# Second up layer as seven quarter products, with DMA-made low halves and a deadline-ordered schedule, in an attention and two feed-forward layers kernel

## Chip, cores and metric

The kernel runs on one core of a Trainium2 chip. The metric is the device time of one execution in microseconds (us). Three runs of the kernel before took 534.87 to 536.11 us, with a median of 535.9 us. Engines are named as in the profile: PE is TensorE, DVE is VectorE, ACT is ScalarE, POOL is GpSimd, SP is SyncE, whose queue issues the plain DMAs.

## Reference

Attention with capped scores over 24 heads, then two feed-forward layers on 896 tokens of width 768, with 2048 hidden units each. All is in float32.

```python
scores = cap * tanh(q @ k.T / sqrt(64) / cap)       # 2 x 12 heads, 448 x 448, head_dim 64
x = softmax(scores) @ v                             # then tokens x 768
h = x @ w1; x = (max(h, 0) + alpha * min(h, 0)) @ w2    # first layer
h = x @ w3; out = max(h, 0) ** 2 @ w4                   # second layer
```

## The kernel before

Weights come from HBM as 64-bit floats and are rebuilt in 32 bits: ACT scales the high words (line 251), and DVE masks, shifts and joins the low words (lines 256, 258, 249). Where `half` is set, ACT does a part of it by a pass over the low words (line 245, on 16-bit halves), which takes the place of DVE's line 258.

TensorE multiplies in a rounded 32-bit format. For enough digits each operand is split into a high part h (ACT, line 275, rounds) and a low part l (DVE, line 276 or 277, what is left), and each product is three matmuls: h x h, h x l, l x h (line 210). All of these have 128 rows of weights and 448 columns of tokens, one of the two batches. `up_now` (line 218) already makes three blocks of the first up layer for one batch at the end of attention.

An up layer is a plain product: 16 blocks of 128 hidden units x 2 batches x 6 chunks x 3 matmuls. A down layer uses Winograd's form of Strassen's method. Weights and tokens are cut into 2 x 2 quarters (the two batches are halves of the tokens, the hidden units and outputs are halved too), and seven products of quarters P1 to P7 take the place of eight, at the price of sums: S1 to S4 of weight quarters, T1 to T4 of token quarters, and additions of the results. T4 and S4 are made by DMAs that accumulate into their destination, issued from POOL (`gather`, line 270).

The order of the work after attention is written out by a planner. `Plan.op` records every operation with an estimated cost, what it reads and what it writes. `Plan.order` then plays them through: whenever an engine is free, it starts the ready operation that was recorded first (lines 109, 125), if the buffers that it needs are free. Buffers come from pools by tag (`SLOTS`): `raw` for incoming weights, `w` for rebuilt weights, `wh` and `wl`, `xh` and `xl` for the split pieces, `g` for tokens, `ps` for PSUM banks. The result of the first layer goes into the tile `x` (`put`), high and low parts apart.

Of the kernel before, what the change touches and what calls it, by code (L numbers as in the profile page):

```python
# [32 lines left out]
PLAIN = ()  # L33

HALF = (lambda f, first: False, lambda i, a: i % 2 == 0)

SQ = lambda f: False

LAND = 9.0

SHIFT = 40

SHIFT_DOWN = 40

SLOTS = {"raw": 2, "w": 16, "wh": 3, "wl": 3, "g": 35, "t": 1, "xh": 4, "xl": 4}


class Buf:

    def __init__(self, tag=None, tile=None):  # L50
        self.tag, self.tile = tag, tile
        self.left, self.writer, self.readers, self.taken = 0, None, [], tag is None

# [9 lines left out]
class Plan:  # L63
# [4 lines left out]
    def tag(self, name, tiles):  # L68
        self.free[name], self.queue[name] = list(tiles), []

    def op(self, engine, cost, emit, reads=(), writes=(), port=False, lag=0.15):
# [7 lines left out]
        for other in set(before):  # L79
            if other is not None and other is not op:  # L80
                other.feeds.append(op)
                op.needs += 1
        for buf in reads:
            buf.readers.append(op)
        for buf in writes:
            buf.writer, buf.readers = op, []
            if not buf.taken:
                buf.taken = True
                op.takes.append(buf)
                self.queue[buf.tag].append(op)  # L90
        op.bufs = list(dict.fromkeys([*reads, *writes]))
        for buf in op.bufs:
            buf.left += 1

    def order(self):
        import heapq

        ready = {e: [] for e in {op.engine for op in self.ops}}
# [5 lines left out]
        while events:  # L104
            now = events[0][0]
            while events and events[0][0] <= now:
                _, _, what, op = heapq.heappop(events)
                if what == "ready":
                    heapq.heappush(ready[op.engine], (op.number, op))
                elif what == "end":  # L110
                    for buf in op.bufs:
                        buf.left -= 1
                        if not buf.left and buf.tag:
                            self.free[buf.tag].append(buf.tile)
# [5 lines left out]
            while moved:  # L120
                moved = False
                for e, waiting in ready.items():
                    if idle[e] > now:
                        continue
                    for item in sorted(waiting):
                        op = item[1]
                        if op.port and port > now:
                            continue
                        if any(self.queue[b.tag][0] is not op or not self.free[b.tag] for b in op.takes):
                            continue  # L130
                        for b in op.takes:
                            b.tile = self.free[b.tag].pop(0)
                            self.queue[b.tag].pop(0)
# [23 lines left out]
class Net:  # L157
# [47 lines left out]
    def multiply(self, ps, w, x, c, first, last, more=False):  # L205
        if len(w) == 1:
            self.nc.tensor.matmul(ps, w[0][:, c, :], x[0], start=first and not more, stop=last, skip_group_check=more)
# [23 lines left out]
    def load(self, src, half, sign=1):  # L231

        nc, plan, n = self.nc, self.plan, self.NC * P
        raw, w = Buf("raw"), Buf("w")
# [37 lines left out]
    def split(self, w, tags, n, sign=1):  # L272
        nc, plan = self.nc, self.plan
        h, l = (Buf(t) for t in tags)
        plan.op("ACT", self.act(n), lambda: nc.scalar.mul(h.tile, w.tile, -1.0) if sign < 0 else nc.scalar.copy(h.tile, w.tile), [w], [h])  # L275
        plan.op("DVE", self.dve(n), lambda: nc.vector.scalar_tensor_tensor(l.tile, w.tile, -1.0, h.tile.bitcast(F32), op0=ALU.mult, op1=ALU.subtract)
                if sign < 0 else nc.vector.tensor_sub(l.tile, w.tile, h.tile.bitcast(F32)), [w, h], [l], port=True)  # L277
        return h, l

    def products(self, ps, w, x, c, first, last, more=False):  # L280
        self.plan.op("PE", 3 * 0.2038 if len(w) == 2 else 0.746, lambda: self.multiply(ps.tile, [b.tile for b in w], [b.tile for b in x], c, first, last, more),
                     [*w, *x], [ps])

    def up(self, w, f, b, first):
# [3 lines left out]
        minus = b == 0 and f >= half  # L288
        for c in range(self.NC):
            self.products(ps, w, self.x[b, c], c, c == 0, c == self.NC - 1)  # L290
        if first or not minus:
            plan.op("ACT", self.act(S), lambda: nc.scalar.activation(g.tile, ps.tile, AF.Relu), [ps], [g])  # L292
        if first:
            plan.op("ACT", self.act(S), lambda: nc.scalar.activation(t.tile, ps.tile, AF.Relu, scale=-1.0), [ps], [t])
            slope = self.slope_t if minus else self.minus_t
            plan.op("DVE", self.dve(S), lambda: nc.vector.scalar_tensor_tensor(  # L296
                g.tile, t.tile, slope[:, f:f + 1], g.tile, op0=ALU.mult, op1=ALU.subtract if minus else ALU.add), [t, g], [g], port=True)
        else:
            if minus:
                plan.op("ACT", self.act(S), lambda: nc.scalar.mul(g.tile, ps.tile, -1.0), [ps], [g])  # L300
                plan.op("DVE", self.dve(S) + 0.06, lambda: nc.vector.scalar_tensor_tensor(
                    g.tile, ps.tile, 0.0, g.tile, op0=ALU.max, op1=ALU.mult), [g, ps], [g])
            elif SQ(f):
                plan.op("ACT", self.act(S), lambda: nc.scalar.square(g.tile, g.tile), [g], [g])
            else:
                plan.op("DVE", self.dve(S) + 0.06, lambda: nc.vector.scalar_tensor_tensor(
                    g.tile, ps.tile, 0.0, g.tile, op0=ALU.max, op1=ALU.mult), [g, ps], [g])
# [4 lines left out]
    def quarter(self, name, i):  # L312
        a = {"A11": 0, "S3": 1, "A12": 2, "A22": 3}[name]
        w = self.a[name, i] = self.load(self.wdown[:, a * PARTS + i], HALF[1](i, a), -1 if a == 2 else 1)
# [3 lines left out]
    def factor(self, name, i, plain):  # L318
# [8 lines left out]
        elif name == "S4":  # L327
            a[name, i] = a.pop(("A12", i))
            self.gather(a[name, i], a["S2", i])
        return (a[name, i],) if plain else self.split(a[name, i], ("wh", "wl"), n, -1 if name in ("S4",) else 1)  # L330

    def tokens(self, name, k, plain):
# [6 lines left out]
        elif name == "T4":  # L339
            self.gather(g[0, half + k], g[1, k])  # L340
# [530 lines left out]
```

## Time and profile before

| | |
|---|---|
| median of 3 runs | 535.9 us |
| profiled execution, its own time | 535.74 us |
| its span, first to last instruction | 534.0 us |
| PE busy | 517.3 us, 97% |
| DVE busy | 452.5 us, 85% |
| ACT busy | 343.0 us, 64% |
| granted TensorE clock | 0.999 of full speed |

The busy time of an engine is a share of the whole span; stages with different limits are mixed in it, so the section with rows below has a table by stage. A matmul's bar is longer than the distance to the next start, since matmuls overlap; the same holds for DVE and ACT when their queues are full. The distance between starts is then the price of an instruction.

### The profile page before, as it was taken

The numbers are of one execution on the slowest core, as the hardware profiler recorded it, in microseconds if no ns is written. First come the engines' busy times: TensorE is split into PE (matmuls) and PEld (weight loads), VectorE is DVE, ScalarE is ACT, GpSimd is POOL, SyncE is SP. The second block draws the span as 40 slices with busy tenths as digits, with TensorE's granted clock in tenths as the row PEclk, the third lists the DMA queues.
The fourth block names the chain that finished last, engine by engine and source line by source line (L and its number), as shares of the span: only waits on it lengthen the run. The fifth ranks groups of instructions, "written<-read, shape, count | busy, mean of one in ns | idle before, by whom it ended". The sixth has DMA issues, their size and how long they took to land.

```text
span 534.0 us, 7022 instructions
## 1 busy us (share of the span) xinstructions
PE 517.3 (97%) x2604; PEld 432.3 (81%) x2604; DVE 452.5 (85%) x639; ACT 343.0 (64%) x468; POOL 23.1 (4%) x36
## 2 busy tenths in 40 slices
PE   7889999999999999999999999999999999999995
PEld 2223335889999999789999989999999999999994
DVE  1598999878888989999999996987898999987661
ACT  5999994265568677975766734447756675556560
POOL 1000000000000000025000000000000001600000
PEclk9999999999999999999999999999999999999999
DMA  6545441044654455479201355556554500930111
GB/s 179 216 163 198 140 130 53 23 131 160 229 182 128 168 163 196 130 210 223 49 2 64 115 166 189 177 178 184 173 165 152 191 24 11 199 101 1 53 52 58
DMA packets 23034, 71.07 MB, mean 133 GB/s; under 512 B 4304, under 2 KB 13008, under 8 KB 22992
## 3 DMA queue, kind: packets, MB, share of 16 engines
q1 hardware_dynamic: 19392, 63.72, 36.4%
q0 software_dynamic: 3456, 6.82, 7.1%
q8 instruction: 22, 0.36, 0.3%
q14 instruction: 20, 0.16, 0.1%
q10 hardware_dynamic: 144, 0.00, 0.0%
HBM read 60.89 MB, written 2.79 MB: 119 GB/s over the span
## 4 chain that ended last, share of the span: by engine, by line
PE 67%; DVE 19%; ACT 8%; issue 3%; DMA 2%; POOL 0%; SPq 0%; DVEq 0%; ACTq 0%; POOLq 0%
PE hm L210 56%; PE pv L554 4%; PE ps L504 3%; DVE wl L277 3%; ACT raw L245 2%; DVE w L249 2%; PE ps L210 2%; DVE raw L258 2%; DVE xl L277 2%; ACT E L519 2%; DVE g L265 1%; ACT E L524 1%; DVE g L296 1%; DVE raw L256 1%; DMA v<-in_vT 1%
## 5 line engine op out<-in xcount | busy, mean ns | idle before, releaser
L210 PE MATMUL hm<-x,wh 128*128 128x448 f32 x732 | 205.5, 362 | 0.7 <-DVE x L352 0.5
L210 PEld LDWEIGHTS hm<-x,wh 128*128 128x128 f32 x732 | 137.2, 187 | 10.6 <-DVE x L352 0.8
L210 PE MATMUL hm<-x,wl 128*128 128x448 f32 x366 | 132.9, 363 | 0.6 <-DVE wl L277 0.6
L210 PE MATMUL hm<-xh,wh 128*128 128x448 f32 x336 | 122.2, 364 | 1.0 <-ACT g L361 1.0
L210 PE MATMUL hm<-xl,wh 128*128 128x448 f32 x336 | 122.2, 364 | 0.7 <-DVE xl L277 0.7
L210 PE MATMUL hm<-xh,wl 128*128 128x448 f32 x336 | 121.8, 363 | 0.0
L275 ACT CAST xh<-g 128x448 fp32r<-128x448 f32 x90 | 51.1, 569 | 53.6 <-PE hm L210 43.2
L277 DVE TENSOR_TENSOR wl<-w,wh 128x768 fp32r<-128x768 f32 x77 | 73.3, 952 | 5.9 <-ACT wh L275 4.8
L251 ACT ACTIVATE w<-raw 128x768 f32<-128x768 f32 x61 | 55.9, 916 | 33.2 <-DMA raw<-in_w 29.1
L275 ACT CAST wh<-w 128x768 fp32r<-128x768 f32 x77 | 64.4, 836 | 14.4 <-PE hm L210 10.7
L210 PEld LDWEIGHTS hm<-x,wl 128*128 128x128 f32 x366 | 68.7, 188 | 5.5 <-DVE wl L277 1.0
L249 DVE SCALAR_TENSOR_TENSOR w<-w,raw 128x768 int32<-128x768 int32 x61 | 58.1, 954 | 12.6 <-ACT raw L245 11.9
L210 PEld LDWEIGHTS hm<-xh,wh 128*128 128x128 f32 x336 | 63.1, 188 | 6.3 <-ACT g L361 2.0
L210 PEld LDWEIGHTS hm<-xl,wh 128*128 128x128 f32 x336 | 63.1, 188 | 5.8 <-DVE xl L277 1.7
L210 PEld LDWEIGHTS hm<-xh,wl 128*128 128x128 f32 x336 | 63.1, 188 | 4.2
L277 DVE TENSOR_TENSOR xl<-g,xh 128x448 fp32r<-128x448 f32 x90 | 55.3, 619 | 11.1 <-ACT xh L275 10.1
L292 ACT ACTIVATE g<-hm 128x448 f32<-128x448 f32 x53 | 29.4, 554 | 23.1 <-PE hm L210 23.1
L258 DVE SCALAR_TENSOR_TENSOR raw<-raw 128x768 int32<-128x768 int32 x45 | 42.9, 956 | 1.0
L519 ACT ACTIVATE E<-ps,scale_t 128x896 f32<-128x896 f32 x42 | 40.2, 1023 | 4.4 <-PE ps L504 4.3
L524 ACT ACTIVATE E<-E,cap_t 128x1792 f32<-128x1792 f32 (+1 forms) x24 | 38.2, 1620 | 0.0
L504 PE MATMUL ps<-q,k 64*128 64x448 f32 x132 | 30.4, 571 | 4.9 <-DVE rows L579 2.3
L245 ACT ACTIVATE raw<-raw 128x768 f16<-128x768 f32 x16 | 31.3, 1955 | 5.7 <-DVE raw L253 5.7
(89 smaller groups left out, 454.1 us busy)
## 6 DMA issues: line engine op xcount, KB each, us to landing
raw<-in_w SPq DMA_DIRECT2D x64, 768.0 KB, 4.2
g<-g POOLq DMA_DIRECT2D x16, 224.0 KB, 5.4
w<-w POOLq DMA_DIRECT2D x8, 384.0 KB, 6.2
out_T<-g SPq DMA_DIRECT2D x12, 224.0 KB, 2.0
k<-in_kT SPq DMA_DIRECT2D x11, 224.0 KB, 5.0
q<-in_qT SPq DMA_DIRECT2D x11, 224.0 KB, 5.5
v<-in_vT SPq DMA_DIRECT2D x6, 384.0 KB, 5.2
rb<-row SPq DMA_DIRECT2D x10, 224.0 KB, 3.7
```

The source lines that it names most:

```text
L210: self.nc.tensor.matmul(ps, a[:, c, :], m, start=first and n == 0 and not more, stop=last and n == 2, skip_group_check=more)
L245: nc.scalar.mul(halves[:, :, :, 1], parts()[1].bitcast(F32), sign * 2.0 ** -60)
L249: nc.vector.scalar_tensor_tensor(bits, bits, 3, parts()[0], op0=ALU.logical_shift_left, op1=ALU.bitwise_or)
L251: plan.op("ACT", self.act(n) + 0.06, lambda: nc.scalar.mul(w.tile, parts()[1].bitcast(F32), 2.0 ** -112), [high, raw], [w])
L258: plan.op("DVE", self.dve(n), lambda: nc.vector.scalar_tensor_tensor(parts()[0], parts()[0], 29, parts()[1], op0=ALU.logical_shift_right, ...
L275: plan.op("ACT", self.act(n), lambda: nc.scalar.mul(h.tile, w.tile, -1.0) if sign < 0 else nc.scalar.copy(h.tile, w.tile), [w], [h])
L277: if sign < 0 else nc.vector.tensor_sub(l.tile, w.tile, h.tile.bitcast(F32)), [w, h], [l], port=True)
L292: plan.op("ACT", self.act(S), lambda: nc.scalar.activation(g.tile, ps.tile, AF.Relu), [ps], [g])
L504: nc.tensor.matmul(ps[:, e, :], k[rows, c * P:c * P + P], q[rows], start=True, stop=True)
L519: nc.scalar.activation(es[-1][:, n % 2], ps, AF.Tanh, scale=self.scale_t)
L524: self.nc.scalar.activation(x, x, AF.Exp, scale=self.cap_t)
L554: nc.tensor.matmul(self.pv[u][rows, g, :], self.v[u][0][:, g, c, rows], self.chunk(u, g * FULL + c)[:, e], start=c == 0, stop=False)
```

## The change

The second up layer becomes seven products of quarters too (`squares`, `all_squares`), for each pair of a block and the block half the layer further on. The weights come in an order that fits (`quads`), and their quarters are combined on DVE (`weights`), but for the first sum of seven of the eight pairs, which is an accumulating DMA. The input of that layer is no longer put as is: `take` makes T1 to T4 and splits all seven token factors.

In `split`, a new way `far` makes the low half without DVE: ACT writes the rounded h and -x, also rounded, and an accumulating DMA adds x to it. T1 and T2 of both down layers go this way (`FAR`), and the four pieces of weight quarter A12 in the second (`FARW`). In the second down layer, T4 and S4 are sums on DVE (`T4`, `S4`).

The 16 raw blocks of the second up layer use ACT's low-word pass (`HALF`). There are three raw buffers; the scratch of software-made DMAs is 4096 bytes; buffers `cell` hold either a weight or two token halves, and the token pieces of the down layers use the slots of `x`.

The planner first plays the operations backwards in time (`rank`, `backwards`); the time at which each one would have to be done gives its place in the order, where the place in the recording stood before.

```diff
-HALF = (lambda f, first: False, lambda i, a: i % 2 == 0)
-LAND = 9.0
-SLOTS = {"raw": 2, "w": 16, "wh": 3, "wl": 3, "g": 35, "t": 1, "xh": 4, "xl": 4}
+GATHER = lambda k: k > 0
+HALF = (lambda f, first: not first, lambda i, a: i % 2 == 0)
+T4 = {False: True, True: False}
+S4 = {False: True, True: False}
+FAR = lambda final, name, k: name in ("T1", "T2")
+FARW = lambda final, name, i: final and name == "A12"
+SQUARE = lambda b, f: "ACT" if b else "DVE"
+LAND = 7.5
+SLOTS = {"raw": 3, "w": 9, "wh": 5, "wl": 5, "g": 35, "t": 1, "cell": 9}
...
     def order(self):
+        self.rank()
...
-                    heapq.heappush(ready[op.engine], (op.number, op))
+                    heapq.heappush(ready[op.engine], (op.rank, op.number, op))
...
-    def split(self, w, tags, n, sign=1):
+    def split(self, w, tags, n, sign=1, port=True, reads=None, far=False):
+        if far and sign > 0:
+            plan.op("ACT", self.act(n), lambda: nc.scalar.copy(h.tile, w.tile), reads, [h])
+            plan.op("ACT", self.act(n), lambda: nc.scalar.mul(l.tile, w.tile, -1.0), reads, [l])
+            self.gather(l, w)
+            return h, l
...
+    def take(self, name, j, x):
+        if name == "B12":
+            b11, b22, u = kept["B11", j], kept["B22", j], Buf("g")
+            plan.op("DVE", self.dve(S), lambda: nc.vector.tensor_sub(b11.tile, x.tile, b11.tile), [x, b11], [b11])
+            factor("T1", b11)
+            plan.op("DVE", self.dve(S), lambda: nc.vector.tensor_sub(u.tile, x.tile, b22.tile), [x, b22], [u])
+            factor("T3", u)
+            self.sum(b22, b22, b11, "tensor_sub", S)
+            factor("T2", b22)
+        else:
+            kept[name, j] = x
+            factor(name, x, 1 if name == "B21" else -1)
+            if name == "B21":
+                self.sum(x, x, kept["B22", j], "tensor_sub", S)
+                factor("T4", x)
+    def weights(self, src, k):
+        u0 = self.load(src[:, 2 * k], HALF[0](2 * k, False), -1)
+        u1 = self.load(src[:, 2 * k + 1], HALF[0](2 * k + 1, False))
+        a11, a12, a21, a22 = Part(u0, 0), Part(u0, 1), Part(u1, 0), Part(u1, 1)
+        if GATHER(k):
+            self.gather(a21, a11)
+        else:
+            self.sum(a21, a21, a11, "tensor_add", n // 2)
+        pairs["P1"] = pairs["P2"] = self.split(u0, ("wh", "wl"), n, reads=[a11, a12], far=DISTANT(k, "P1"))
+        pairs["P7"] = pairs["P4"] = self.split(u1, ("wh", "wl"), n, reads=[a21, a22], far=DISTANT(k, "P7"))
+        self.sum(a21, a21, a22, "tensor_add", n // 2)
+        pairs["P6"] = self.split(a21, ("wh", "wl"), n // 2)
+        self.sum(a12, a12, a21, "tensor_add", n // 2)
+        self.sum(a11, a21, a11, "tensor_sub", n // 2)
+        pairs["P5"] = pairs["P3"] = self.split(u0, ("wh", "wl"), n, reads=[a11, a12], far=DISTANT(k, "P5"))
+    def squares(self, k):
+        for name in ("P1", "P6", "P5", "P7", "P2", "P4", "P3") if LATE(k) else ("P1", "P2", "P6", "P5", "P7", "P4", "P3"):
+            c, at, b, more = parts[name]
+            p = ps[c]
+            for j in range(J):
+                self.products(p, self.pairs[k][name], self.factors[b, j], at * J + j, j == 0, j == J - 1, more)
+            if name in ("P1", "P6", "P7"):
+                keep(name, p)
...
-        self.raw = const.tile([P, 2, self.NC, P], I64, name="raw")
+        self.raw = const.tile([P, 3, self.NC, P], I64, name="raw")
...
-    nc = bacc.Bacc("TRN2", target_bir_lowering=False, num_devices=1)
+    nc = bacc.Bacc("TRN2", target_bir_lowering=False, num_devices=1, dynamic_dma_scratch_size=4096)
```

Three places show how instructions move. The first is DVE in the middle of the second up layer, before. `wl` is the low part of a weight block, `raw` and `w` are incoming and rebuilt weights, `hm` are PSUM banks and `g` the results.

```order
L306 SCALAR_TENSOR_TENSOR g4_795<-hm3_831,g4_795 128x448
L256 TENSOR_SCALAR raw_62<-raw_62 128x768
L306 SCALAR_TENSOR_TENSOR g6_797<-hm5_833,g6_797 128x448
L258 SCALAR_TENSOR_TENSOR raw_62<-raw_62 128x768
L249 SCALAR_TENSOR_TENSOR w10_785<-w10_785,raw_62 128x768
L256 TENSOR_SCALAR raw_62<-raw_62 128x768
L258 SCALAR_TENSOR_TENSOR raw_62<-raw_62 128x768
L277 TENSOR_TENSOR wl1_107<-w1_776,wh1_104 128x768
L306 SCALAR_TENSOR_TENSOR g3_794<-hm2_830,g3_794 128x448
```

And DVE in the same layer, now, with quarters of 384 columns:

```order
L374 SCALAR_TENSOR_TENSOR w4_783<-w4_783,raw_62 128x768
L499 TENSOR_TENSOR g22_810<-g22_810,hm0_823 128x448
L390 TENSOR_TENSOR w4_783<-w3_782,w4_783 128x768
L412 TENSOR_TENSOR wl3_111<-w0_779,wh3_106 128x768
L492 SCALAR_TENSOR_TENSOR g22_810<-g22_810 128x448
L412 TENSOR_TENSOR wl1_109<-w2_781,wh1_104 128x768
L518 SCALAR_TENSOR_TENSOR g24_812<-hm4_827,g24_812 128x448
L499 TENSOR_TENSOR g26_814<-g26_814,hm5_828 128x448
L499 TENSOR_TENSOR g20_808<-g20_808,hm0_823 128x448
L412 TENSOR_TENSOR wl0_108<-w6_785,wh0_103 128x768
L390 TENSOR_TENSOR g18_806<-g24_812,g18_806 128x448
L390 TENSOR_TENSOR w6_785<-w6_785 128x384
```

Where a block had one instruction on its result and one on its low part, there are now sums of weight quarters (line 390, 384 columns), joins of products (line 499) and squares (lines 492, 518) beside the low parts; the instruction of line 258 is gone from the blocks of this layer.

The second place is POOL's queue in the first down layer and after it. These are its accumulating DMAs before, from the last T4 on.

```order
L270 DMA g25_816<-g10_801 128x448
L270 DMA g27_818<-g12_803 128x448
L270 DMA w6_781<-w0_775 128x768
L270 DMA w7_782<-w2_777 128x768
L270 DMA w8_783<-w4_779 128x768
L270 DMA w9_784<-w0_775 128x768
L270 DMA g0_791<-g1_792 128x448
```

And now from the same T4 on; `x` are the slots of token pieces, here their low halves.

```order
L395 DMA g25_813<-g10_798 128x448
L395 DMA g27_815<-g12_800 128x448
L395 DMA x_63<-g0_788 128x448
L395 DMA x_63<-g1_789 128x448
L395 DMA x_63<-g2_790 128x448
L395 DMA x_63<-g4_792 128x448
L395 DMA x_63<-g6_794 128x448
L395 DMA x_63<-g8_796 128x448
```

Sixteen low halves of T2 and T1 are put behind the T4 in POOL's queue, and two of the four weight pieces of S4 come between the last of them.

The third place is PE where the two layers meet. Before, the last product of the first layer ran to its end, and the second layer's input `x` came after it. This is now; `cx` are token factors in `cell` buffers.

```order
L335 MATMUL hm4_827<-x_63,wl3_111 128x448
L335 MATMUL hm6_829<-x_63,wh3_106 128x448 x2
L335 MATMUL hm6_829<-x_63,wl3_111 128x448
L335 MATMUL hm7_830<-cx_2239,wh4_107 128x448 x2
L335 MATMUL hm7_830<-cx_2239,wl4_112 128x448
L335 MATMUL hm7_830<-cx_2252,wh4_107 128x448 x2
L335 MATMUL hm7_830<-cx_2252,wl4_112 128x448
L335 MATMUL hm7_830<-cx_2268,wh4_107 128x448 x2
L335 MATMUL hm7_830<-cx_2268,wl4_112 128x448
L335 MATMUL hm0_823<-cx_2355,wh2_105 128x448 x2
```

The first product of the second layer (into `hm7`) reads factors that were ready before; the next one (into `hm0`) reads a factor that `take` makes from the first layer's late results.

## Rows read from the trace of the kernel before

**Rows 1.** The page's head: span, busy time, share and instructions of an engine.

```profile
span 534.0 us, 7022 instructions
PE 517.3 (97%) x2604; PEld 432.3 (81%) x2604; DVE 452.5 (85%) x639; ACT 343.0 (64%) x468; POOL 23.1 (4%) x36
```

**Rows 2.** Busy time by stage: stretch, its length, busy us and instructions of each engine.

```profile
core 0: us, PE busy (x) PEld busy (x) DVE busy (x) ACT busy (x) POOL busy (x), PEclk, DMA share, GB/s
0.00:100.90 100.90, 93.49 (x499) 38.09 (x500) 79.94 (x98) 80.22 (x75) 2.02 (x12) 1.00 0.44 145
100.90:220.00 119.10, 118.50 (x593) 110.75 (x591) 104.27 (x145) 79.53 (x122) 0.00 (x0) 1.00 0.49 159
220.00:312.70 92.70, 90.24 (x444) 82.33 (x442) 91.76 (x143) 62.06 (x99) 10.63 (x12) 1.00 0.45 117
312.70:412.00 99.30, 99.30 (x496) 93.10 (x497) 84.49 (x120) 56.18 (x74) 0.00 (x0) 1.00 0.53 173
412.00:527.60 115.60, 115.60 (x578) 108.03 (x576) 91.13 (x136) 65.02 (x101) 10.42 (x12) 1.00 0.30 76
```

**Rows 3.** Timeline of PE: start, duration, line, operation, matmuls merged.

```profile
100.89 0.56 PE L210 MATMUL hm<-x,wh 128*128 128x448 f32 x2
...
517.64 0.36 PE L210 MATMUL hm<-xl,wh 128*128 128x448 f32 x1
...
527.44 0.36 PE L210 MATMUL hm<-xh,wl 128*128 128x448 f32 x1
```

**Rows 4.** The page's groups: the two layers' matmuls, count, busy, mean ns.

```profile
L210 PE MATMUL hm<-x,wh 128*128 128x448 f32 x732 | 205.5, 362 | 0.7 <-DVE x L352 0.5
L210 PE MATMUL hm<-x,wl 128*128 128x448 f32 x366 | 132.9, 363 | 0.6 <-DVE wl L277 0.6
L210 PE MATMUL hm<-xh,wh 128*128 128x448 f32 x336 | 122.2, 364 | 1.0 <-ACT g L361 1.0
L210 PE MATMUL hm<-xl,wh 128*128 128x448 f32 x336 | 122.2, 364 | 0.7 <-DVE xl L277 0.7
L210 PE MATMUL hm<-xh,wl 128*128 128x448 f32 x336 | 121.8, 363 | 0.0
```

**Rows 5.** Timeline of PE at two holes; in brackets idle time and releaser.

```profile
231.03 0.47 PE L210 MATMUL hm<-xl,wh 128*128 128x448 f32 x1 [0.65 <-DVE xl L277]
...
312.68 0.47 PE L210 MATMUL hm<-x,wh 128*128 128x448 f32 x1 [0.55 <-DVE x L352]
```

**Rows 6.** Timeline of DVE with a full queue.

```profile
261.62 0.62 DVE L265 TENSOR_TENSOR early<-g,g 128x448 f32<-128x448 f32 x1
262.16 0.95 DVE L277 TENSOR_TENSOR wl<-w,wh 128x768 fp32r<-128x768 f32 x1
263.03 0.62 DVE L277 TENSOR_TENSOR xl<-early,xh 128x448 fp32r<-128x448 f32 x1
```

**Rows 7.** Timeline of ACT with a full queue.

```profile
225.09 0.59 ACT L275 CAST xh<-g 128x448 fp32r<-128x448 f32 x1
225.56 0.86 ACT L275 CAST wh<-w 128x768 fp32r<-128x768 f32 x1
226.30 0.59 ACT L275 CAST xh<-g 128x448 fp32r<-128x448 f32 x1
...
230.69 1.95 ACT L245 ACTIVATE raw<-raw 128x768 f16<-128x768 f32 x1
232.38 0.90 ACT L275 CAST wh<-w 128x768 fp32r<-128x768 f32 x1
```

**Rows 8.** Accumulating DMAs: packets and MB, POOL's issue, time to landing of those on tokens.

```profile
q0 software_dynamic: 3456, 6.82, 7.1%
L270 POOL DMA_DIRECT2D g<-g x16 | 14.8, 966 | 8.6 <-DVE xl L277 7.6 <-issue 1.0
DMA to landing us min/median/max: 4.6/5.4/7.2
```

**Rows 9.** Waits in the second layer: total us, times, longest us.

```profile
DVE w L249 <- ACT raw L245: 8.6, 7, 2.0
```

More of the change, by code (lines that the diff above doesn't have):

```diff
@@ L89, in op, with rank @@
                 op.takes.append(buf)
-                self.queue[buf.tag].append(op)
+                self.queue[QUEUES.get(buf.tag, buf.tag)].append(op)
         op.bufs = list(dict.fromkeys([*reads, *writes]))
+        op.bufs += dict.fromkeys(b.whole for b in op.bufs if isinstance(b, Part))
         for buf in op.bufs:
             buf.left += 1
+    def rank(self):
+        count = {n: len(t) for n, t in self.free.items()}
+        claims, users = {}, {}
+        for op in self.ops:
+            op.later = list(op.feeds)
+            for b in op.bufs:
+                users.setdefault(id(b), []).append(op)
+        for op in self.ops:
+            for b in op.takes:
+                n = sum(count[p] for p in POOLS.get(b.tag, (b.tag,)) if p != "half")
+                c = claims.setdefault(b.tag, [])
+                if len(c) >= n > 0:
+                    for other in users[id(c[-n])]:
+                        if other.number < op.number:
+                            other.later.append(op)
+                c.append(b)
+        self.backwards()
@@ new lines, in backwards @@
+    def backwards(self):
+        import heapq
+        before = {}
+        for op in self.ops:
+            op.rank, op.open = 0.0, len(op.later)
+            for o in op.later:
+                before.setdefault(o, []).append(op)
+        now = {e: 0.0 for e in ("PE", "DVE", "ACT", "POOL", "SP")}
+        waiting = [(0.0, -op.number, op) for op in self.ops if not op.open]
+        heapq.heapify(waiting)
+        ready = {e: [] for e in now}
+        due = {op: 0.0 for op in self.ops}
+        left, time = len(self.ops), 0.0
+        events = [(0.0, -1)]
+        while left:
+            while waiting and waiting[0][0] <= time:
+                op = heapq.heappop(waiting)[2]
+                heapq.heappush(ready[op.engine], (-op.number, op))
+            for e, r in ready.items():
+                if r and now[e] <= time:
+                    op = heapq.heappop(r)[1]
+                    span = 1.8 if e == "SP" else op.cost
+                    now[e] = time + span
+                    op.rank = -(time + op.cost)
+                    left -= 1
+                    for o in before.get(op, ()):
+                        due[o] = max(due[o], time + op.cost + o.lag)
+                        o.open -= 1
+                        if not o.open:
+                            heapq.heappush(waiting, (due[o], -o.number, o))
+            times = [t for t in now.values() if t > time]
+            if waiting:
+                times.append(max(waiting[0][0], time + 1e-9))
+            time = min(times)
@@ L206, in multiply @@
         if len(w) == 1:
-            self.nc.tensor.matmul(ps, w[0][:, c, :], x[0], start=first and not more, stop=last, skip_group_check=more)
+            self.nc.tensor.matmul(ps, w[0][:, c, :], x[0], start=first, stop=last)
             return
@@ L287, in up @@
         ps, g, t = Buf("ps"), Buf("g"), Buf("t")
-        minus = b == 0 and f >= half
+        minus = T4[False] and b == 0 and f >= half
         for c in range(self.NC):
             self.products(ps, w, self.x[b, c], c, c == 0, c == self.NC - 1)
[L291 to L307, printed above, removed]
@@ L357, in down @@
         kept, chains = {}, {}
+        self.ring = "z" if final else "x"
         def keep(name, j, ps):
```

258 lines of the change are left out of this document (188 added, 70 removed).

## Prediction

> **What bounds the kernel now.** I read the profile from the top: the busy shares, then a table by stage, then the matmuls' own starts, then what fills VectorE and ScalarE. TensorE is busy 97% of a span of 534.0 us and VectorE 85% [rows 1]. The table by stage says where each matters [rows 2]. The first 100.9 us are attention. From there to 312.7 us runs the first feed-forward layer, to 527.6 us the second, and the last 6.4 us write the output. In the second layer TensorE is full (99.3 of 99.3 us, 115.6 of 115.6) while VectorE works 84.5 + 91.1 = 175.6 of 214.9 us and ScalarE 56.2 + 65.0 = 121.2. Between 220 and 312.7 us it is the other way round: VectorE is busy 91.8 of 92.7 us and TensorE has gaps.
>
> A busy TensorE can still be slower than its peak, so I take the pace from the starts. From the matmul at 517.64 us to the one at 527.44 us there are 49 steps [rows 3]: 9.80 / 49 = 0.200 us each. The two layers hold 732 + 366 + 3 x 336 = 2106 of them [rows 4], which is 421.2 us without a gap. They start at 100.89 us and the last one ends its step at 527.64 us, 426.75 us later. So 5.5 us are holes: by the counts of the stages almost all lie before 312.7 us (444 matmuls are 88.8 of 92.7 us). Two of them show their cause: TensorE waits for VectorE's low half of a token piece at 231.03 us, and for the next layer's input at 312.68 us [rows 5].
>
> **The change, part by part.** *Matmuls.* The second up layer was 16 blocks x 2 batches x 6 chunks x 3 = 576 matmuls. As seven products it is 8 pairs x 7 x 3 chunks x 3 = 504. Nothing else changes their number: 2106 - 72 = 2034. That is 72 x 0.200 = 14.4 us off the path that sets the end, since TensorE is full in that layer.
>
> *VectorE.* By the built order, from before to after, instructions on 448 columns go up by 13, those on 768 go down by 8, and 33 on 384 columns are new. The price of one in a full queue is the distance between starts, 0.535 us for 448 columns and 0.87 us for 768 [rows 6]; 384 columns were not run before, and the straight line through the two gives 0.47 (ends: 0.43, in proportion to 448 columns, and 0.535, the 448-column price itself). Sum: 7.0 - 7.0 + 15.5 = +15.5 us. Split by place: the first layer loses 16 low halves of token pieces to DMAs (-8.6 us), but where 12 low halves were made for the next layer's input, there are now 21 and 12 sums (33 against 12, +11.2 us). The second layer gets 8 x 0.535 - 8 x 0.87 + 33 x 0.47 = +12.8 us. It saves 16 instructions on 768 columns (raw weights are now joined with ScalarE's help) and 16 low halves, and pays for sums and splits of weight quarters, joins and squares.
>
> *ScalarE.* 57 more on 448 columns, 12 more on 768, 8 on 384, and 16 more passes that shift the low word of raw weights. Starts lie 0.47, 0.74 and 1.69 us apart [rows 7], 0.40 estimated for 384: 27 + 9 + 3 + 27 = +66 us, of which 32 x 0.47 + 9 + 3 + 27 = 54 us fall in the second layer.
>
> So in the second layer, where the work takes 214.9 - 14.4 = 200.5 us of TensorE, VectorE needs 175.6 + 12.8 = 188.4 us and ScalarE 121.2 + 54 = 175. All of this lies beside the matmuls as long as no queue runs empty waiting for another. The cover shrinks, though: VectorE's idle time there goes from 39.3 us to 12.1 us, and the transition's 11.2 us come right in front of it.
>
> *Accumulating DMAs.* There were 24 and are now 55; 36 of these make the low half of a piece (ScalarE writes -x, rounded, and the DMA adds x). Those of before on 448 columns took 4.6 to 7.2 us from issue to landing, 5.4 in the middle, and GpSimd 0.97 us to issue [rows 8]. The kind with a rounded destination isn't in the trace; its bounds are those 4.6 and 7.2 us, and I take 5.4. On the path it costs nothing: the token pieces go round in a ring of 24 slots, 12 pieces of a high and a low half, and each piece is read by 9 matmuls, so a slot comes free 11 x 9 = 99 matmuls, 20 us, before TensorE reads what is put there next. ScalarE's two steps (0.94 us), the issue and the landing are 7.3 us. Even 12 us more would be hidden; beyond that each late piece would hold TensorE by its whole excess.
>
> The scratch for these DMAs shrinks to 4096 bytes. The trace has 3456 packets for the 24 of before [rows 8], 144 each, 9 on each of 16 DMA engines; by the built order each waits for the eighth before it, so eight are in flight at most. [...]
>
> *Third raw buffer, attention.* One weight load can start earlier. The first 100.9 us are full with attention's own work (TensorE 93.5, ScalarE 80.2 us) [rows 2]; I take 0, with ends of 0 and -7.4 us (all that TensorE isn't busy there).
>
> *New order.* The holes can go either way. Those between 220 and 312.7 us arise with a full VectorE, which now has 8.6 us less to do there: I expect 1.5 of the 3.9 us to stay. In the second layer VectorE goes from 82% to 94% (188.4 / 200.5), and the transition makes its first part fuller still. When VectorE was as full as 99%, TensorE lost 3.9 us in 92.7 us. At half that rate, 200.5 us lose 4.2 us; I take 4.5. With 0.5 us at the start: 6.5 us of holes in place of 5.5. Ends: 0 and 12 us (the full-VectorE rate over the whole second layer, 8.4 us, and the 3.9 us unchanged).
>
> **The sum.** The profiled execution took 535.74 us, 1.7 us beyond its span, and the median of the runs is 535.9 us, practically the same, so I count from 535.9: - 14.4 (72 matmuls) + 1.0 (holes 6.5 for 5.5) = 522.5 us.
>
> **The rivals.**
> First, the new order closes the holes. All three engines have less work than TensorE in each layer, which speaks for it; that VectorE has only 12 us left speaks against it. With 0 to 4 us of holes: 535.9 - 14.4 - 5.5 = 516.0 up to 520 us.
>
> Second, and on the other side: VectorE becomes the second layer's bound through its waits for ScalarE's low-word pass. Such a pass takes two steps of a full VectorE, and the join of the same weights stands behind it in VectorE's queue. In the second layer of before VectorE waited for it 7 times, 8.6 us in all, 1.2 us each [rows 9], with 8 passes; now there are 24 (all 16 blocks of the second up layer, 8 of the down layer). If each still costs 1.1 us, that is 26 us, plus 11.2 us spilled over from the transition, against 12.1 us of idle time: 25 us of new holes, 521.5 + 25 = 546 us. It makes the kernel slower from 14.4 us of new holes on, which is 0.64 us of waiting per pass. For it: 1.2 us was paid where VectorE had 39 us to spare. Against: a wait that fills otherwise idle time is not a price, and the new order sorts by when a result is due, so other work can stand between. A half-way form, 6 to 13 us of new holes, gives 528 to 534 us.
>
> Third, the change of scratch doesn't leave the DMAs free: each would wait for the one before. The low halves are due every 9 matmuls, 1.8 us, and one after another they would take 5.4 + 1 us: 32 x 4.6 = 147 us less two leads of 20 us, 107 us, so 629 us. [...]
>
> **How the numbers follow.** My forecast (4 to 12 us of holes, 520 to 528 us) has 0.52; closed holes (516 to 520, a little under if attention gains) 0.24; the half-way form 0.12; the second rival in full 0.07; the third 0.02; and 0.03 is left for a result within 0.3% of 535.9 us (534.3 to 537.5), which is about what a measurement can tell from no change. So faster 0.52 + 0.24 + 0.12 = 0.88, same 0.03, slower 0.09. The range from 516 to 530 us leaves out the slow cases and a third of the half-way form.
>
> **What would show it right or wrong.** In the profile after, 2034 matmuls of the two layers, 0.200 us apart in the full stretches; VectorE near 468 us and ScalarE near 410 us busy; landing of the low halves near 5 us, and no wait of TensorE for a DMA. Holes are to lie in the 50 us after the layers meet, with a wait for VectorE. If TensorE loses over 12 us there, and VectorE's longest waits are for the low-word pass, the second rival holds. If gaps lie between GpSimd's DMAs in the first down layer, or TensorE waits for them, it is the third. A span below 514 us would mean that attention itself got shorter, which I count as nothing.

## The result and the profile after

The changed kernel takes 523.1 us (median of 4 runs, 522.25 to 524.66) where the kernel before takes 536.0: a ratio of 0.976, 95% interval 0.972 to 0.980. The forecast was 522.5 us. The profiled execution after took 523.51 us with a span of 521.6.

The page's head of the changed kernel, which answers to [rows 1]:

```profile
span 521.6 us, 7032 instructions
PE 505.3 (97%) x2532; PEld 419.1 (80%) x2532; DVE 459.8 (88%) x677; ACT 402.8 (77%) x561; POOL 51.4 (10%) x67
```

TensorE has 72 instructions less, ScalarE works 59.8 us longer, VectorE only 7.3 us. By stage, in the stretches of [rows 2] (stretch, its length, busy us and instructions of each engine, granted clock, share of the DMA engines, GB/s):

```profile
0.00:100.90 100.90, 93.45 (x498) 37.88 (x499) 80.06 (x98) 79.64 (x75) 2.02 (x12) 1.00 0.47 153
100.90:220.00 119.10, 119.10 (x597) 111.36 (x595) 110.62 (x157) 91.37 (x136) 0.00 (x0) 1.00 0.57 186
220.00:312.70 92.70, 89.30 (x445) 82.98 (x444) 84.38 (x135) 78.66 (x123) 27.14 (x30) 1.00 0.65 141
312.70:412.00 99.30, 98.46 (x474) 88.99 (x474) 94.95 (x151) 81.17 (x111) 4.71 (x5) 0.98 0.51 153
```

Attention is as long as it was. VectorE does 110.6 us of work between 100.9 and 220 us instead of 104.3, and has less in the stretch after it. The pace and the holes come from the starts of the two layers' matmuls; here they are by form, with count, least, median and longest duration in ns, and first and last start:

```profile
L335 PE MATMUL hm<-x,wh x1212: 360/362/576, 101.0 to 516.4; 128*128 128x448 f32 x174
L335 PE MATMUL hm<-x,wl x606: 360/363/575, 101.4 to 516.6; 128*128 128x448 f32 x152
L335 PE MATMUL hm<-cx,wh x144: 360/363/474, 306.4 to 420.3; 128*128 128x448 f32 x144
L335 PE MATMUL hm<-cx,wl x72: 360/363/525, 306.8 to 420.5; 128*128 128x448 f32 x72
```

The four counts add up to 2034. From 101.0 us to the end of the last step at 516.8 are 415.8 us; 2034 x 0.200 are 406.8, so 9.0 us are holes, against 5.5 before. Slower steps count as holes here. After the last start there are 5.0 us until the span ends, 6.6 before [rows 1, 3]. Together: -14.4 (matmuls) + 3.5 (holes) - 1.6 (tail) + 0.1 (a later start) = -12.4 us, which is the difference of the spans.

Of the two holes of [rows 5] the first is gone: TensorE is busy 20.00 of 20 us in each window from 220 to 300 us. Where the layers meet there is a larger one. PE's timeline there (start, duration, line, operation, in brackets idle time and releaser):

```profile
308.00 0.36 PE L335 MATMUL hm<-cx,wl 128*128 128x448 f32 x1
309.89 0.67 PE L335 MATMUL hm<-cx,wh 128*128 128x448 f32 x2 [1.52 <-ACT wh L410]
312.44 0.47 PE L335 MATMUL hm<-cx,wl 128*128 128x448 f32 x1 [1.88 <-DVE wl L412]
...
314.82 0.57 PE L335 MATMUL hm<-x,wl 128*128 128x448 f32 x1
315.19 0.95 PE L335 MATMUL hm<-x,wh 128*128 128x448 f32 x2
```

TensorE lacks the first weight blocks of the second up layer, then runs with steps of 0.37 us instead of 0.20 until 317.3 us. In the windows of 2 us from 312 us on the granted clock is 0.95, 0.50 and 0.70, and 1.00 again from 318 us, with no gap left after 312.44 us.

```profile
312.00:314.00 2.00, 1.56 (x7) 1.48 (x8) 2.00 (x4) 0.48 (x2) 0.00 (x0) 0.95 0.00 0
314.00:316.00 2.00, 2.00 (x7) 1.75 (x7) 2.00 (x4) 0.24 (x1) 0.00 (x0) 0.50 0.00 0
316.00:318.00 2.00, 2.00 (x9) 1.82 (x8) 2.00 (x4) 0.80 (x2) 0.88 (x1) 0.70 0.86 246
```

So some 3.8 us of gaps and 1.6 us of slow steps, 5.4 of the 9.0 us, lie within 12 us of the meeting at 306.4 us. VectorE is busy 19.9 of 20 us from 280 to 300 us. But before that it stood still, as these windows show:

```profile
240.00:260.00 20.00, 20.00 (x101) 18.75 (x100) 18.23 (x27) 18.12 (x33) 14.02 (x16) 1.00 1.11 213
260.00:280.00 20.00, 20.00 (x101) 18.75 (x100) 13.59 (x21) 17.54 (x23) 0.97 (x2) 1.00 0.69 175
```

VectorE is idle 8.2 of these 40 us. The longest wait, 3.7 us, is for a raw weight load, which was issued at 258.61 us and took 9.5 us to land, where the median of all loads is 4.3. The other 4.5 us are waits for ScalarE, which makes h and -x of each piece whose low half a DMA finishes and is busy 18.1 and 17.5 of 20 us here. VectorE's timeline:

```profile
263.96 0.62 DVE L411 SCALAR_TENSOR_TENSOR x<-g,x 128x448 fp32r<-128x448 f32 x1
268.24 0.56 DVE L378 TENSOR_SCALAR raw<-raw 128x768 int32<-128x768 int32 x1 [3.66 <-DMA raw<-in_w]
```

From 240 to 260 us, up to the issue of that load, GpSimd is at work on 16 accumulating DMAs, and the DMA engines' share is 1.11. The queue and the landing of the DMAs on tokens, answering to [rows 8]:

```profile
q0 software_dynamic: 7920, 13.70, 15.1%
L395 POOL DMA_DIRECT2D x<-g x28 | 25.5, 1110 | 19.7 <-ACT x L403 17.1 <-DVE w L374 0.9 <-issue 0.7
DMA to landing us min/median/max: 3.1/5.1/10.0
```

### The profile page after: what moved, and what is told of

It is laid out like the page before. It is cut to its first block, busy times and chain, and to the rows that moved or that the text cites. A ratio compares the mean times of both kernels' runs of the same rounds, so it can differ in the third digit from the quotient of the medians.

```text
span 521.6 us, 7032 instructions
## 1 busy us (share of the span) xinstructions
PE 505.3 (97%) x2532; PEld 419.1 (80%) x2532; DVE 459.8 (88%) x677; ACT 402.8 (77%) x561; POOL 51.4 (10%) x67
## 4 chain that ended last, share of the span: by engine, by line
PE 40%; DVE 33%; ACT 14%; issue 7%; DMA 6%; POOL 0%; DVEq 0%; ACTq 0%; POOLq 0%
PE hm L335 31%; DVE wl L412 5%; ACT raw L370 4%; DMA raw<-in_w 4%; DVE x L412 4%; DVE raw L383 3%; PE pv L797 3%; DVE w L374 3%; DVE g L390 3%; PE ps L335 2%; ACT w L376 2%; DVE cw L390 2%; PE ps L747 2%; ACT wh L410 2%; DVE g L541 2%
## 5 line engine op out<-in xcount | busy, mean ns | idle before, releaser
L335 PE MATMUL hm<-x,wh 128*128 128x448 f32 x1212 | 342.3, 363 | 0.7 <-ACT g L487 0.7
L335 PEld LDWEIGHTS hm<-x,wh 128*128 128x128 f32 x1212 | 227.6, 188 | 18.1 <-ACT g L487 2.6
L335 PE MATMUL hm<-x,wl 128*128 128x448 f32 x606 | 220.1, 363 | 0.0
L335 PEld LDWEIGHTS hm<-x,wl 128*128 128x128 f32 x606 | 114.1, 188 | 8.0 <-DVE wl L412 0.3
L370 ACT ACTIVATE raw<-raw 128x768 f16<-128x768 f32 x32 | 62.9, 1965 | 3.2 <-DVE raw L378 2.9
L410 ACT CAST x<-g 128x448 fp32r<-128x448 f32 x77 | 41.8, 567 | 10.9 <-DVE g L390 9.3
L412 DVE TENSOR_TENSOR x<-g,x 128x448 fp32r<-128x448 f32 x77 | 47.4, 618 | 0.3 <-ACT x L410 0.2
L335 PE MATMUL hm<-cx,wh 128*128 128x448 f32 x144 | 41.1, 366 | 1.7 <-ACT wh L410 1.5
L390 DVE TENSOR_TENSOR g<-g,g 128x448 f32<-128x448 f32 x55 | 33.3, 619 | 0.1
L747 PEld LDWEIGHTS ps<-q,k 64*128 64x128 f32 x132 | 10.9, 185 | 23.9 <-ACT E L762 11.2
L797 PE MATMUL pv<-E,v 128*64 128x448 f32 x144 | 29.5, 546 | 0.1
```

The source lines that it names most:

```text
L335: self.nc.tensor.matmul(ps, a[:, c, :], m, start=first and n == 0 and not more, stop=last and n == 2, skip_group_check=more)
L370: nc.scalar.mul(halves[:, :, :, 1], parts()[1].bitcast(F32), sign * 2.0 ** -60)
L390: plan.op("DVE", self.dve(n), lambda: getattr(nc.vector, op)(out.tile, a.tile, b.tile), [a, b], [out], port=True)
L410: plan.op("ACT", self.act(n), lambda: nc.scalar.mul(cut(h), w.tile, -1.0) if sign < 0 else nc.scalar.copy(cut(h), w.tile), reads, [h])
L412: if sign < 0 else nc.vector.tensor_sub(cut(l), w.tile, cut(h).bitcast(F32)), [*reads, h], [l], port=port)
L747: nc.tensor.matmul(ps[:, e, :], k[rows, c * P:c * P + P], q[rows], start=True, stop=True)
```

## The experiments

My theory after the result (A): the hole at the meeting comes from the accumulating DMAs of the first down layer, which delay the raw load, so that VectorE idles and is late afterwards. Its rival (B): VectorE simply has too much to do there. Beside that, each part of the change was undone alone. "Holes" is worked out as above from the starts in each run's profiled execution; that was the fastest of its runs for e1 (519.8 us) and e3 (534.9 us) and the slowest for e8 (525.2 us) and e11 (538.8 us), so a difference of 2 or 3 us in this column alone says little.

| run | edit | us | ratio to before (95%) | holes, us |
|---|---|---|---|---|
| changed kernel | | 523.1 | 0.976 (0.972 to 0.980) | 9.0 |
| e1 | no DMAs for low halves, first down layer | 521.2 | 0.975 (0.970 to 0.979) | 5.9 |
| e2 | VectorE makes them instead | 523.9 | 0.976 (0.974 to 0.979) | 8.9 |
| e3 | plain second up layer | 537.4 | 1.004 (1.001 to 1.007) | 6.4 |
| e4 | order as written | 543.0 | 1.014 (1.011 to 1.017) | 26.1 |
| e5 | half the DMAs, passes alternate | 519.5 | 0.970 (0.968 to 0.972) | 5.6 |
| e6 | no low-word pass, second up layer | 526.9 | 0.983 (0.980 to 0.985) | 12.4 |
| e7 | two raw buffers | 535.3 | 0.999 (0.998 to 1.001) | 20.3 |
| e8 | no DMAs for T1, T2 at all | 523.9 | 0.977 (0.974 to 0.979) | 11.2 |
| e9 | e5 with later up weights | 519.5 | 0.969 (0.967 to 0.971) | 4.7 |
| e10 | before with three raw buffers | 535.2 | 0.9972 (0.9949 to 0.9995) | 5.5 |
| e11 | e7 and e6 together | 536.8 | 1.000 (0.999 to 1.002) | 23.7 |
| e12 | scratch of 512 bytes | 602.1 | 1.122 (1.119 to 1.125) | 88.4 |

**e1, the DMAs left out.**

```
-            self.gather(l, w)
+            if self.ring == "x":
+                plan.op("POOL", 1.3, lambda: None, [w, l], [l], lag=LAND)
+            else:
+                self.gather(l, w)
```

> The changed kernel in its order, with 32 accumulating DMAs left out: those that finish the low halves of T1 and T2 pieces in the first down layer (the low half stays -x, so the result is another one). VectorE's and ScalarE's instructions stay the same. Theory A (the hole of 5.5 us where the layers meet comes from these DMAs: a raw weight load issued at 258.6 us takes 9.5 us to land beside them, VectorE idles 8 us between 240 and 280 us and runs late after that): raw loads land in under 6 us there, VectorE is busy over 18.5 of each 20 us from 240 to 280, the hole is under 2 us, time 517 to 520 us. Theory B (VectorE simply has too much to do before the layers meet, the late load hides nothing else): the hole stays 4 to 6 us, time 522.5 to 524.5 us.

Sixteen DMAs are left out, half of the 32 that the expectation names: those of the second down layer stay. The loads issued between 240 and 300 us land in 3.9 to 6.2 us, the one at 258.2 us in 3.9. One gap is left where there were two, and the granted clock is 1.00 in each window of 20 us from 220 to 440 us:

```profile
310.15 0.47 PE L335 MATMUL hm<-cx,wl 128*128 128x448 f32 x1 [1.87 <-DVE wl L415]
```

Holes are 3.1 us smaller, all of it where the layers meet. But the time, between the two expectations, can't be told from the changed kernel's (the intervals overlap), and VectorE still idles 6.3 us between 240 and 280, now waiting for ScalarE alone:

```profile
240.00:260.00 20.00, 20.00 (x101) 18.75 (x101) 17.97 (x27) 17.75 (x32) 0.86 (x1) 1.00 0.40 91
260.00:280.00 20.00, 20.00 (x101) 18.74 (x101) 15.75 (x25) 19.08 (x25) 0.86 (x1) 1.00 0.41 133
```

That these DMAs slowed this load is shown. That they cost about 3 of the 5.4 us is what the two traces suggest; the times don't show it. That all of VectorE's idling came from the load was wrong.

**e2, VectorE makes the 16 low halves of the first down layer; e8, all 32.**

```
-FAR = lambda final, name, k: name in ("T1", "T2")
+FAR = lambda final, name, k: final and name in ("T1", "T2")    # e2
+FAR = lambda final, name, k: False                             # e8
```

> VectorE makes the 16 low halves of T1 and T2 again in the first down layer (DMAs only in the second): +8.6 us of VectorE work before the layers meet, 16 DMAs less. Theory A: no late load, VectorE keeps 8 us that it idled and spends them on the 8.6: hole about as large, 522 to 525 us. Theory B: the 8.6 us come on top of a full queue: hole 5.5 + 6 to 9 us, time 529 to 532 us.

> All 32 low halves of T1 and T2 pieces are made by VectorE again (the four weights' low halves stay with DMAs): VectorE +32 x 0.535 = 17.1 us, 32 DMAs less. With the DMAs only in the second down layer the time was 523.9 us. If the DMAs of the second down layer also bring nothing (VectorE was busy 88.5 of 103 us there): 522.5 to 525 us. If they carry VectorE's work before 440 us, as 16 x 0.535 = 8.6 us: 528 to 533 us.

Both took 523.9 us. In e2 VectorE works 20.00 of 20.00 us in each window from 240 to 300 us: it spends the 8 us that it idled. What B forecast for e2 did not happen, and the 32 DMAs, as they are placed, are worth nothing that these runs can show. The 8.9 us of holes in e2 are not those of the changed kernel, though: 2.6 instead of 5.5 us lie between 306 and 320 us, and 4.4 instead of 2.3 between 340 and 380. In e8 VectorE is busy 99 instead of 90 us after 412 us; 0.8 us of its holes lie there.

**e3, the second up layer as a plain product.**

```
-                self.all_squares()
+                for f in range(self.NF):
+                    w = self.split(self.load(src[:, f], HALF[0](f, first), 1, "u"), ("wh", "wl"), self.NC * P)
+                    for b in both:
+                        self.up(w, f, b, False)
```

(this edit also has `up` squaring the relu in that layer, a plain split in place of the sums of `take`, the weights in the old arrangement, and no early start of two pairs of weights in the first down layer)

> The second up layer as 16 blocks x 2 batches x 18 matmuls again (576 in place of 504), all else as changed. If the 72 matmuls carry the gain, as in the prediction's sum: +14.4 us and less VectorE work at the layers' meeting (12 low halves in place of 21 and 12 sums), so 3 to 5 us of hole less: 532 to 536 us. If the new order, the DMAs and the third buffer carry a part of the gain: under 530 us.

It took 14.3 us more than the changed kernel, 1.4 us above the range expected if the 72 matmuls carry the gain, and is no faster than the kernel before. The other parts together bring nothing without the seven products. VectorE works 36.7 us less here (423.1 us busy), so this isn't the price of 72 matmuls alone, and the ten runs spread from 534.9 to 541.7 us.

**e4, the order by when an operation is written.**

```
-                    heapq.heappush(ready[op.engine], (op.rank, op.number, op))
+                    heapq.heappush(ready[op.engine], (op.number, op.number, op))
```

> The changed kernel, but among ready operations of an engine the one written first goes first, as before, and not the one due first. If the order by due times is what keeps VectorE's waits for ScalarE's low-word pass short (8.0 us in 9 waits): more holes, 8 to 20 us, 528 to 540 us, with long waits of VectorE for that pass. If the order matters little: 522 to 525 us.

19.9 us slower, and 1.4% slower than before. Of VectorE's waits one has grown most (line waited for: total us, times, longest); these are its row and those of the low-word pass:

```profile
DVE wl L412 <- ACT wh L410: 17.9, 14, 3.4
...
DVE w L374 <- ACT raw L370: 3.1, 6, 1.4
...
DVE cw L374 <- ACT raw L370: 2.4, 2, 1.6
```

VectorE waits 17.9 us for the rounded high halves of weights, 3.4 in the changed kernel. The waits for the low-word pass, which the expectation named, are 5.5 us, less than the 8.0 of the changed kernel. But neither is where the time goes. Of the 17.9 us, 14.5 fall between 260 and 280 us and after 440 us, where TensorE has no gap. The largest holes lie where VectorE is full, around the starts of the two down layers: 7.0 of the 26.1 us between 200 and 220 us, 8.3 between 420 and 440 us. The second of these three rows is a stretch of the long waits:

```profile
200.00:220.00 20.00, 15.46 (x67) 13.39 (x66) 19.62 (x30) 14.58 (x24) 0.00 (x0) 0.91 0.57 197
260.00:280.00 20.00, 20.00 (x101) 18.75 (x101) 12.72 (x20) 18.02 (x29) 5.91 (x7) 1.00 0.75 155
420.00:440.00 20.00, 13.88 (x60) 11.89 (x59) 19.62 (x30) 14.94 (x19) 0.00 (x0) 0.91 0.55 192
```

In the first and the third TensorE waits 10.6 us, 7.3 of them for the low halves of token pieces. This is one of them, on ScalarE, VectorE and TensorE:

```profile
433.16 0.64 ACT L410 CAST x<-g 128x448 fp32r<-128x448 f32 x1
434.08 1.82 DVE L374 SCALAR_TENSOR_TENSOR cw<-cw,raw 128x768 int32<-128x768 int32 x2
435.82 0.55 DVE L378 TENSOR_SCALAR raw<-raw 128x768 int32<-128x768 int32 x1
436.29 0.61 DVE L412 TENSOR_TENSOR x<-g,x 128x448 fp32r<-128x448 f32 x1
436.96 0.74 PE L335 MATMUL hm<-x,wh 128*128 128x448 f32 x1 [2.40 <-DVE x L412]
```

The high half is there at 433.8 us, but VectorE first joins two weight blocks and shifts a third, which the recording has earlier (`quarter` stands before `down`), and TensorE stands still meanwhile. In the changed kernel no matmul of the two layers waits for the low half of a token piece.

**e6, the low-word pass taken out of the second up layer.**

```
-HALF = (lambda f, first: not first, lambda i, a: i % 2 == 0)
+HALF = (lambda f, first: False, lambda i, a: i % 2 == 0)
```

> ScalarE's low-word pass is taken out of the second up layer; VectorE masks and joins those 16 blocks by itself: 16 instructions on 768 columns more, 16 x 0.87 = 13.9 us, ScalarE 16 x 1.69 = 27 us less. If VectorE's work is what is short from 300 to 412 us (19 of each 20 us busy): 8 to 14 us of new holes, 531 to 537 us. If waits for the pass cost as much as the pass saves (the prediction's second rival in small): 520 to 525 us.

3.8 us slower, between the two expectations: of the 13.9 us that the pass takes off VectorE, 3.8 us reach the end.

**e7, two raw buffers; e10, the kernel before with three; e11, two buffers and no pass.**

```
-            plan.tag("raw", [self.raw[:, (AHEAD + n) % 3] for n in range(3)])
+            plan.tag("raw", [self.raw[:, (AHEAD + n) % 3] for n in range(2)])
```

(e7; e11 has the line of e6 as well; e10 makes two buffers three in the kernel before and the 16 slots `w` 14)

> The two layers use two of the three raw buffers (attention keeps three). The prediction counted the third at 0: 521 to 525 us. Rival: each raw buffer is held for its load (4.4 us), VectorE's shift, ScalarE's pass (1.7 us) and VectorE's join, and with two of them VectorE's queue waits for loads: VectorE waits for raw loads over 10 us in all, 527 to 536 us.

> The kernel before with a third raw buffer alone (two slots for joined weights less, 14 for 16). In the changed kernel the third buffer is worth 12.2 us. If it is worth that by itself (ScalarE waited 29.1 us for raw loads in the kernel before): faster, down to 530.5 us, which is all of the 5.5 us of holes. If it matters only where VectorE is full (the changed kernel's meeting of the layers and second up layer): 534 to 537 us.

> Two raw buffers and no low-word pass in the second up layer. Each alone cost 12.2 and 3.8 us. If the pass (1.7 us of ScalarE on the raw words) is what holds a raw buffer too long: the two together cost less than the two added, 527 to 533 us. If raw buffers are held by VectorE's full queue: without the pass VectorE has 13.9 us more to do and they are held longer, the costs add up or more, 538 to 546 us.

The third buffer is worth 12.2 us in the changed kernel and about 1 us in the one before, whose holes stay at 5.5 us. What it does is seen long before the holes. This is the first up layer of e7, to be held against the second row by stage above:

```profile
100.90:220.00 119.10, 119.10 (x597) 111.63 (x597) 103.51 (x144) 82.54 (x125) 0.00 (x0) 1.00 0.48 154
```

TensorE is full in both. With two buffers VectorE does 7.1 us less for the weights of the layer to come, and the DMA engines bring 154 instead of 186 GB/s, some 3.8 MB less; the loads that SyncE issued before 220 us are 26 instead of 31. That work comes back where VectorE has no room; it is busy 19.97 of 20 us from 300 to 320 us. TensorE waits for it, and in the last row for a copy on ScalarE that stands behind casts of what VectorE makes late:

```profile
289.56 0.47 PE L335 MATMUL hm<-x,wh 128*128 128x448 f32 x1 [0.46 <-DVE x L411]
305.04 0.47 PE L335 MATMUL hm<-x,wh 128*128 128x448 f32 x1 [0.87 <-DVE x L412]
307.51 0.71 PE L335 MATMUL hm<-x,wh 128*128 128x448 f32 x1 [0.99 <-DVE x L412]
318.76 1.12 PE L335 MATMUL hm<-cx,wh 128*128 128x448 f32 x2 [3.58 <-ACT early L487]
```

The granted clock is 0.86 from 300 to 320 us, and of the 20.3 us of holes some 4 are slow steps. e7's time is what the rival expected, but its sign is not there: VectorE waits 4.8 us for raw loads, not over 10. In the kernel before, a third buffer moves the same work forward (110.2 us of VectorE in that stretch, 104.3 without it), and little comes of it, as the second expectation of e10 had it; its second layer has 39 us of VectorE to spare. In e11 the buffer costs 9.9 us without the pass (536.8 against 526.9) and 12.2 with it: the pass isn't the main thing that holds buffers. Neither expectation of e11 was met; it lies 2.3 us under the sum of the two costs.

**e12, an eighth of the scratch.**

```
-dynamic_dma_scratch_size=4096
+dynamic_dma_scratch_size=512
```

> The changed kernel with 512 bytes of scratch for the accumulating DMAs in place of 4096. If the scratch doesn't hold these DMAs back: 522 to 524.5 us, landing 5 to 9 us as before. If it does (the prediction's third rival): GpSimd's issues lie further apart, low halves land later, over 527 us. [...]

This is the third rival of the prediction, 79 us slower than the changed kernel. GpSimd's timeline; the second line is the first low half:

```profile
261.29 0.88 POOL L395 DMA_DIRECT2D g<-g  x1 [2.50 <-issue]
264.62 0.87 POOL L395 DMA_DIRECT2D x<-g  x1 [2.46 <-issue]
268.00 0.88 POOL L395 DMA_DIRECT2D x<-g  x1 [2.51 <-issue]
```

One is issued every 3.4 us and lands after 3.1 us (median): one at a time. In the changed kernel eight low halves are issued between 237.98 and 245.43 us:

```profile
237.98 7.44 POOL L395 DMA_DIRECT2D x<-g  x8
```

With 512 bytes the first of them is issued at 264.62 us, 26.6 us later, since ten other accumulating DMAs stand before it, issued 3.3 to 6.5 us apart. TensorE waits for what they bring, 18.9 us for the first one:

```profile
PE hm L335 <- DMA x<-g: 58.8, 25, 18.9
```

The size of the scratch is the only edit, so 512 bytes hold these DMAs back: one every 3.4 us, where with 4096 bytes eight are issued in 7.44 us.

**e5 and e9, a faster version.** e1 and e2 suggest that between 16 DMAs and none there is a better number.

```
-FAR = lambda final, name, k: name in ("T1", "T2")
-HALF = (lambda f, first: not first, lambda i, a: i % 2 == 0)
+FAR = lambda final, name, k: name in (("T1", "T2") if final else ("T1" if k % 2 == 0 else "T2",))
+HALF = (lambda f, first: not first, lambda i, a: (i + a) % 2 == 0)
-EARLY = {"P5": 0, "P4": 1}     # e9 alone
+EARLY = {"P5": 0, "P3": 1}
```

> A candidate: in the first down layer every other piece of T1 and of T2 gets its low half by a DMA (8 in place of 16), and ScalarE's low-word pass falls on alternate blocks of the down weights, (i + a) even, in place of i even. Theory A (the 16 DMAs there bring nothing because they delay a raw load; half of them leaves the loads free and still takes 4.3 us off VectorE): raw loads land in under 6.5 us, no hole over 1 us where the layers meet, 518 to 520.5 us. Theory B (VectorE's total decides): 4.3 us more work for VectorE, 525 to 528 us.

> The alternating candidate (519.5 us, 5.6 us of holes), and the second pair of up weights is prepared one product later in the first down layer (before P3 in place of P4), so that its VectorE work falls behind the rush before the layers meet. If that rush still costs something: 517.5 to 519 us. If the remaining holes lie in the second up layer alone: 519 to 520.5 us, no change.

519.5 us each, 3.6 us under the changed kernel. In e5 raw loads issued between 240 and 300 us land in 4.1 to 4.8 us, and TensorE's longest single wait from 300 to 420 us is 0.8 us; the granted clock is 1.00 in these stretches:

```profile
260.00:280.00 20.00, 20.00 (x101) 18.75 (x101) 17.32 (x28) 19.95 (x27) 0.86 (x1) 1.00 0.50 143
280.00:300.00 20.00, 20.00 (x101) 18.74 (x101) 19.96 (x35) 20.00 (x30) 0.86 (x1) 1.00 0.44 123
300.00:312.70 12.70, 11.85 (x59) 10.77 (x59) 12.70 (x22) 5.41 (x11) 0.00 (x0) 1.00 0.02 3
```

Which of e5's two edits does it was not tested, nor whether the freer loads do it or the eight steps less on ScalarE, for which VectorE had waited. e9 gains nothing more.

## Why the prediction was right, and where it was not

*Matmuls, -14.4 us.* Right: 2034 of them, 0.200 us apart. That e3 gives back 14.3 us, so nearly the same, is partly chance, since it changes VectorE's work too.

*VectorE, +15.5 us.* Half of it in busy time (+7.3). The price for 384 columns was met: two neighbours in the full queue start at 305.82 and 306.29 us, 0.47 apart. One reason for the difference may be that an instruction in a full queue adds its step (0.535 us) to the busy time and one that stands alone its duration (0.62), and more stand in a queue now; this was not tested. ScalarE rose by 59.8 us, forecast 66.

*Accumulating DMAs.* That they cost TensorE nothing was right: no matmul of the two layers waits for one. That they relieve VectorE where it matters was wrong: I took 8.6 us off the first layer for them, and e2 and e8 give the same time without them. They were hidden from TensorE, but not from a raw load (9.5 us with them, 3.9 without, e1), nor from ScalarE, whose two steps for each piece VectorE waited for.

*Scratch.* The sum has no term for the smaller scratch; that it costs nothing was my estimate, and no run shows it by itself, since a larger scratch was not run in the changed kernel. What the trace at 4096 bytes shows is that no matmul of the two layers waits for these DMAs. At 512 bytes one DMA flies at a time: issued every 3.4 us, landing after 3.1 (e12). If the number in flight goes with the size, which was not tried in between, an estimate from these two runs is that 4096 bytes are just enough for eight.

*Third raw buffer, 0.* This step failed: "I take 0, with ends of 0 and -7.4 us". I looked for its worth in attention, where it begins, and it lies in the first up layer, where it lets five more blocks be loaded ahead. Without it the change gains nothing (e7).

*New order, holes 6.5 us.* 9.0 were measured, inside the ends of 0 and 12. The 1.5 us that were to stay in the first down layer are gone, and the 4.5 us put into the second layer came out as 8.8, most of them around the meeting of the layers, where I had put them, and 1.6 us of those by slower steps at a granted clock of 0.50, which the forecast did not have. The forecast took the kernel before's loss at a full VectorE and carried it over, as if the order could move holes by a few us only. It carries 19.9 us (e4): the parts that I priced as small changes of the holes are what keeps the 14.4 us from being lost again. The tail's 1.6 us, which I had not counted, offset part of the 2.5 us by which the holes were larger. So that the forecast came within 0.6 us is partly luck: the matmuls were right, and the rest came out near although two parts that carry 12.2 and 19.9 us had been priced at 0 and at a few us.

*Rivals.* "Holes closed" is what e5 comes to (519.5 us, in its 516 to 520), but not this kernel. The second rival did not happen: in the second layer VectorE waits for the pass 2.8 us in 4 waits, where I had allowed up to 26, and 8.0 us in 9 in the whole program. Taking the pass out costs 3.8 us. Other work stood between, as the argument against it had said. A loss of its size came in e4 by another way: weights ahead of token pieces in a full VectorE queue. These are the rows for the changed kernel from 306 us on, answering to [rows 9]:

```profile
DVE g L602 <- PE hm L335: 13.5, 3, 11.8
DVE w L374 <- ACT raw L370: 2.8, 4, 1.0
DVE raw L378 <- DMA raw<-in_w: 2.1, 1, 2.1
DVE wl L412 <- ACT wh L410: 0.8, 2, 0.6
```

The third rival is real at an eighth of the scratch, but that 602 us lie near the 629 that I had worked out is luck. A DMA takes 3.4 us in its turn and not 6.4, so the same sum would give 32 x 1.6 - 40 = 11 us, not 79. The two leads of 20 us were not there: the ten other DMAs used up the first, and in the second down layer 23 us are lost as well. And TensorE's slower steps (the granted clock is 0.84 from 240 to 260 us, 0.73 from 260 to 280 and 0.71 from 300 to 320), which the sum does not have, cost some 10 us by their starts.

## What to carry to other kernels

When fewer matmuls are bought with more work on other engines, ask what lets that work be done early: a buffer that only moves loads ahead was worth 1 us while VectorE had room and 12 us once it had none. Work handed to DMAs was hidden here from the engine that reads the result and still slowed a load that feeds the others (9.5 us instead of 3.9), so the best number may lie between all and none. An engine's longest wait is not by itself the loss: in e4 it lay where nothing depended on it, and the holes lay where that engine was full with the wrong work first. And a right total doesn't show that the terms were right: undoing each part alone did.

## What the hardware showed unexpectedly

A load of one weight block took 9.5 us behind 16 accumulating DMAs in 20 us, at a DMA share of 1.11, and 3.9 us with most of them left out; the median is 4.3. After two idle times of 1.5 and 1.9 us TensorE's granted clock was 0.50 for some 3.4 us of unbroken work, which cost 1.6 us more. With 512 bytes of scratch, accumulating DMAs of 224 KB were issued one at a time, 3.4 us apart, and landed after 3.1.
